# The last quarter of a hand-ordered command list is put in another order

## The chip, the cores and the metric

The kernel runs on one core of a Trainium2 chip. The metric is the device time of one execution in microseconds (us). The engines are TensorE (PE in the rows; its weight loads are PEld), VectorE (DVE), ScalarE (ACT), GpSimd (POOL) and SyncE (SP), which only issues transfers here. Each works through its own queue in the order in which its instructions were written.

## The reference

Sliding-window attention with a few global keys, for 4 batches of 768 positions and 8 heads of 64, and then a two-layer network on all 3072 tokens: 512 to 2048 and back, with h * tanh(softplus(h)) between them.

```python
scores = scale * np.matmul(q, k.transpose(0, 1, 3, 2))
...
scores = np.where(keep, scores + bias, -1e9)     # 8 global keys, or the last 96
a = np.exp(scores - np.max(scores, axis=-1, keepdims=True))
a = a / (np.sum(a, axis=-1, keepdims=True) + 1e-09)
x = np.matmul(a, v)                              # heads side by side: 3072 x 512
...
h = x @ w_in
g = h * np.tanh(softplus(h))
return g @ w_out
```

## The kernel before

The tokens are worked on in 12 chunks of 256 (ci), and the 2048 hidden columns in 8 blocks of 256 (fp). A command of the network has the number m = 8 ci + fp, from 0 to 95; a command of attention has a number t from 0 to 95 (a chunk's eight pairs of heads and blocks of 128 rows). Each number in full precision is split into a high and a low half in fp16, and products are three matmuls. For the later chunks a product of two 2 x 2 block matrices takes seven block products in place of eight, which needs sums of the operands beforehand and a corner afterwards.

The order of everything is written out by hand: a string PROGRAM of 2153 commands, each a letter, a number and sometimes a stroke. A loop at the end of windowed() emits them one after the other under a manual schedule, so that the string gives each engine's queue. Semaphores make an instruction wait for its operands and for a free buffer. A stroke chooses the other of two engines for the command.

The commands that matter here, for one m:

- i (moe_in, L631; for m of 88 and more moe_in_seven, L602): TensorE multiplies weights and tokens. moe_in_seven fills a bank "ph" first and a bank "sc" after it; there are two buffers of each.
- I with 100 + m (corner_h, L612 to L616): a copy (ScalarE; with stroke VectorE) and four sums on VectorE, which end in the bank "sc".
- j, u, n, r (L638, L642, L646, L650): four functions on ScalarE.
- H (times_h, L655), VectorE: multiplies by h, which for m of 88 and more it reads from the bank "sc". With this the bank comes free.
- J (sums_g, L668 to L670): three sums on VectorE; with stroke on GpSimd.
- z (high_g, L154 or L152): the high half of gt on ScalarE; with stroke VectorE. Z (low_g, L158): the low half on GpSimd; with stroke VectorE. A low half reads two tiles in SBUF.
- o (moe_out, L805; for m = 95 L821): TensorE multiplies gt and the second weights.

Operands of later blocks are prepared by P (whole_w, L698: GpSimd, with stroke VectorE), G (sums_w, L705 to L713: VectorE, with stroke GpSimd), e (high halves: ScalarE, with stroke VectorE) and m (low halves, L158: GpSimd, with stroke VectorE). A chunk ends with I (corner, L841 to L847) and Q (evacuate, L870, L878), and Y stores it from SP. In attention s, t, y, g, p are scores, maxima, exponentials and the two halves, X is a DMA transposition (L502) on SP, W the product with v (L525), and R, T, U, V finish the rows.

The command k is checks(i). checks(0) (L911 to L915) and checks(1) (L917 to L919) are five and three small operations of VectorE on statistics; checks(2) is one more; checks(3) sums all of it with a matmul (L924) and five small operations of VectorE; checks(5) follows on the last row.

Of the kernel before, what the change touches and what calls it, by code (L numbers as in the profile page):

```python
# [14 lines left out]
U16 = mybir.dt.uint16  # L15
# [27 lines left out]
def tile_kernel(ctx, tc, qd, kd, qT, kT, v, n, w_in, w_out, out):  # L43
# [27 lines left out]
    with ExitStack() as st:  # L71
        left = windowed(st, tc, locals())
# [35 lines left out]
def windowed(st, tc, loc):  # L108
# [170 lines left out]
    k0 = mt.tile([P, P], F32, name="e", bufs=4)  # L279
# [629 lines left out]
    def checks(i):  # L909
# [75 lines left out]
        t70 p69' q19 J50' g68' X69 z48' I5 t71 Z48 z50 s64 y70 p68 X68 Q5 j52 u52 t64 H51 y64 n52 J51' Z50' g64' o48 z51' c19' r52 i53 j53 o49 H52 p64' u53 x8  # L985
        t65 y65 g70 a19' b19 n53 d19 i54 v9 g65 r53 J52' s66 p70' o50 Z51' X64 H53 z52 t67 j54 p65 J53' u54 t66 o51 n54 y66 s72 i56 Z52 q20 Y5 z53' a20 r54 X65
        Z53 H54 J54 h9 y67 i55 g67' g66 j56 z54 p67' p66' u56 n56 o52 j55 r56 t72 t73 H56 J56 u55 n55 r55 z56 Z54 y71 c20 W64 X70 H55 W65 W68 W69 X67 o53 g71
        i57 i58 o54 R16 p71 Z56' l9 W67 T16' J55 d20' W70 j57 X66 u57 n57 y72 j58 U16 b20 W66 z55' X71 g72 p72 X72 u58 r57 W71 y73 H57 Z55 R17 i59 J57' s74 g73'
        t74 n58 z57 t75 V16 r58 j59 y74 H58 T17' o55 u59 i60 U17 p73 J58 n59 I6 g74 Q6 r59 s76 o56 Z57 q21 y75 j60 u60 t76 H59 n60 J59 y76 V17 r60 p74' o57 z58
        z59 Z58' a21' H60 i62 t77 g76' y77 Y6 p76' j62 s78 i61 t79 X73 u62 c22 g77' y79 n62 b21 X76 r62 p77' t78 g75 d22' j61 X77 u61 J60' Z59' z60' H62 y78 o58  # L990
        W72 o59 X74 n61 r61 g79 Z60' J62' c21' W77 W76 W73 i63 g78 z62 j63 H61 u63 q23 n63 p78 i64 d21' x9 R18 Z62' r63 X78 p75 o60 j64 J61 p79' z61 u64 n64 H63
        s80 t80 a22' J63 Z61 r64 b22 T18 i66 o61 j66 z63 v10 t81 H64 W78 u66 y81 J64' X79 Z63' i65 W79 X75 y80 n66 W74 g80 j65 u65 r66 U18 h10 W75 g81' z64' q22
        p80' o62 p81 n65 H66 Z64 X81 i67 J66' r65 R19 z66 s82 j67 u67 H65 Z66 V18 l10 t82 t83 J65' i68 n67 y82 g82 c24' d24' r67 j68 u68 s84 t85 H67 o63 p82 t84
        I7 i69 y85 Q7 y84 J67' g85 n68 j69 X80 z65 s86 g84 o64 c23 r68 u69 x10 Z65' p85 X85 v11 n69 T19' H68 y83 t86 z67 o65 r69 p84 J68' U19 Z67' H69 z68 i71
        X84 J69 j71 t87 o66 u71 h11 d23 n71 r71 V19 y86 z69' i70 j70 W80 Z68' W85 H71 o67 g86 l11 a24 p86' a23 P8' J71' y87 i72 g83 u70 b24 p83 n70 r70 Z69' z71
        H70 X82 g87' W81 p87 J70' j72 u72 o68 i73 j73 X83 n72 W83 X86 r72 z70 b23 X87 W84 W82 u73 Z71' R20 H72 n73 r73 o69 T20' G8' Z70' i76 j76 J72' W86 u76
        H73 n76 Y7 z72' U20 e8 o70 V20 W87 i74 Z72' R21 s88 J73' r76 z73' Z73 o71 j74 H76 m8' u74 t89 i75 n74 t88 I8' y89 s90 Q8 J76' t91 g89 r74 z76 p89 o72
        t90 Z76 H74 j75 y91 s92 T21' J74 z74' i77 u75 U21 n75 o73 r75 X89 V21 H75 j77 u77 Z74 g91' n77 r77 P9' p91 H77 J75' y88 i78 g88 t93 p88 G9 j78 i79 x11
        t92 o74 y93 z75' u78 y92 X88 n78 g92' Z75' r78 H78 y90 J77' g93' p92 j79 u79 z77 s94 J78' p93' n79 o75 e9 Z77' r79 X92 t94 z78 i80 g90' H79 j80 u80 n80
        m9' r80 Z78' p90 o76 t95 y94 i81 H80 y95 J79 j81 u81 X93 g95 P10 W89 J80 W88 G10 o77 z79 i83 Y8 o78 n81 z80 p95' e10 Z79' m10 r81 o79 H81 j83 u83 Z80'  # L1000
        n83 r83 i82 X95 W92 J81' H83 W93 W95 I9 g94 Q9 z81 J83' p94 X91 j82 i84 u82 P11' n82 X90 r82 R22 Z81' H82 T22 W91 W90 G11' X94 z83 e11 U22 J82' o80 j84
        W94 i85 u84 m11' n84 P12' G12' z82 r84 R23 T23 j85 V22 u85 o81 e12 Z83' U23 H84 i86 Z82' m12' n85 r85 j86 u86 o82 n86 H85 i87 J84' V23 J85' r86 P111'
        z84 z85 G111 e111 Z84' j87 u87 o83 H86 m111' P13' n87 Z85' G13' i89 r87 I189 H87 j89 J86 e13 m13' u89 z86 J87' o84 n89 i88 Z86' I188 r89 o85 H89 z87 i90
        P14 j88 u88 I190' o86 n88 r88 G14' Y9 J89' Z87' H88 i91 o87 e14 j90 u90 n90 r90 m14' I191' z89 Z89' H90 J88' I10' j91 z88 Q10 u91 Z88 J90' i92 Y10 n91
        r91 H91 i93 I192 I193 z90 j92 u92 n92 Z90' r92 H92 o88 F0 P15 j93 G15' u93 e15 J91 k0 o89 i94 J92' z91 o90 m15 n93 z92 I194' r93 j94 Z91' u94 H93 Z92
        J93' n94 r94 i95 I195' o91 H94 o92 j95 u95 z93' n95 J94' r95 k1 Z93' z94' H95 k3 o93 Z94 z95' o94 k2 Z95' o95 I11 Q11 k5 k4
    """
    with tc.manual_schedule(engines={E.DVE, E.Activation, E.Pool, E.PE, E.SP}):
        for c in PROGRAM.split():
# [154 lines left out]
```

## Time and profile before

| | |
|---|---|
| median of 3 runs | 596.11 us (595.25 to 596.85) |
| the profiled execution | 596.82 us, with a span of 595.0 us |
| TensorE busy | 575.7 us, 97% of the span |
| VectorE, ScalarE, GpSimd busy | 526.7, 508.2 and 337.0 us |
| mean granted clock of TensorE | 0.996 |

The span is the time from the first to the last instruction of the trace. "Granted clock" is the share of TensorE's full clock that it had. Matmuls are pipelined and their ends are modelled, so gaps between them are read from the starts and from the waits. A line in brackets behind a row is idle time of the engine before it, and what ended it.

### The profile page before, as it was taken

To read this page: it belongs to the slowest core of one execution; us is meant where nothing else is said; L and a number is where in the kernel's file an instruction comes from. 1 tells how busy PE (TensorE), PEld (TensorE's weight loads), DVE (VectorE), ACT (ScalarE), POOL (GpSimd) and SP (SyncE) were. 2 spreads that over 40 slices of the span, in tenths; PEclk is the share of its full clock that TensorE was granted. 3 is DMA by queue.
4 is the path that set the end of the run, shared out by engine and by line. 5 is a ranking of instruction groups with operands and counts; after the bars stand their busy time and mean duration, and the time that the engine had idled before them with its cause. 6 is when DMAs were issued, how large, how long until landed. Compare 5 with 4: busy or idle time off the path is not lost.

```text
span 595.0 us, 15592 instructions
## 1 busy us (share of the span) xinstructions
PE 575.7 (97%) x5871; PEld 475.5 (80%) x5871; DVE 526.7 (89%) x1300; ACT 508.2 (85%) x1157; POOL 337.0 (57%) x325
## 2 busy tenths in 40 slices
PE   4999999999999999999999999999999999999987
PEld 3887766666767789888889889888889888889975
DVE  5999999989998998986979988798879899999995
ACT  4999999998999999898888878888998689787861
POOL 0125422244757678677574573424847675877972
PEclk9999999999999999999999999999999999999989
DMA  8999886574555355374764672537444133420001
GB/s 248 317 320 228 163 263 193 147 166 112 135 100 114 68 105 126 69 193 99 116 140 104 129 194 55 107 81 188 85 90 106 21 81 75 72 72 3 36 1 40
DMA packets 133263, 73.80 MB, mean 124 GB/s; under 512 B 102176, under 2 KB 123040, under 8 KB 133184
## 3 DMA queue, kind: packets, MB, share of 16 engines
q1 hardware_dynamic: 132752, 72.50, 51.5%
q8 instruction: 47, 0.77, 0.5%
q10 hardware_dynamic: 432, 0.27, 0.2%
q14 instruction: 32, 0.26, 0.1%
HBM read 38.62 MB, written 6.29 MB: 75 GB/s over the span
## 4 chain that ended last, share of the span: by engine, by line
PE 63%; DVE 15%; ACT 14%; issue 3%; POOL 3%; DMA 2%; SPq 0%; DVEq 0%; ACTq 0%; POOLq 0%
PE ph L631 27%; PE pav L805 10%; PE po L805 7%; PE po L821 6%; PE sc L437 5%; ACT A L460 2%; PE sc L525 2%; PE pav L821 2%; ACT e L646 2%; DVE gf L655 2%; DVE gt L158 2%; ACT e L650 1%; ACT e L642 1%; ACT e L638 1%; DVE A L451 1%
## 5 line engine op out<-in xcount | busy, mean ns | idle before, releaser
L631 PE MATMUL ph<-xT,wts 128*128 128x256 f16 x2112 | 243.0, 273 | 1.3 <-DVE gf L655 1.3
L631 PEld LDWEIGHTS <-wts 128*128 128x128 f16 x2112 | 204.0, 98 | 30.5 <-issue 2.4
L805 PEld LDWEIGHTS <-gt 128*128 128x128 f16 x1491 | 143.7, 98 | 20.3 <-issue 2.6
L460 ACT ACTIVATE A<-A,nm 128x232 f32<-128x232 f32 (+1 forms) x192 | 88.2, 461 | 5.7 <-DVE nm L451 5.6
L158 POOL TENSOR_TENSOR gt<-gf,gt 128x896 f16<-128x896 f32 (+1 forms) x40 | 67.8, 1696 | 40.0 <-ACT gt L154 16.6
L158 POOL TENSOR_TENSOR hl<-A,hl 128x512 f16<-128x512 f32 (+1 forms) x41 | 53.0, 1293 | 49.8 <-ACT hl L154 19.0
L638 ACT ACTIVATE e<-ph 128x512 f32<-128x512 f32 x88 | 51.5, 585 | 28.2 <-PE ph L631 28.0
L451 DVE CUSTOM_DVE_ANT_0 A<-sc,mb 128x232 f32<-128x232 f32 (+1 forms) x192 | 63.6, 375 | 11.9 <-PE sc L437 7.5
L655 DVE SCALAR_TENSOR_TENSOR gf<-e,ph 128x512 f32<-128x512 f32 x88 | 60.1, 682 | 13.2 <-ACT e L650 9.4
L158 DVE TENSOR_TENSOR gt<-gf,gt 128x896 f16<-128x896 f32 (+1 forms) x56 | 66.8, 1193 | 5.5 <-ACT gt L154 5.3
L642 ACT ACTIVATE e<-e,ones 128x512 f32<-128x512 f32 x96 | 68.8, 717 | 1.9
L646 ACT ACTIVATE e<-e,part 128x512 f32<-128x512 f32 x96 | 68.6, 714 | 1.5
L805 PE MATMUL pav<-wts,gt 128*128 128x256 f16 x402 | 66.8, 275 | 0.3 <-DVE gt L158 0.3
L154 ACT ACTIVATE gt<-gf 128x896 f16<-128x896 f32 (+1 forms) x65 | 55.8, 861 | 12.1 <-POOL gf L670 9.4
L668 POOL TENSOR_TENSOR gf<-gf 128x128 f32<-128x128 f32 x53 | 36.6, 690 | 45.1 <-DVE gf L655 41.9
L650 ACT ACTIVATE e<-e 128x512 f32<-128x512 f32 x96 | 59.8, 622 | 1.4
L805 PE MATMUL po<-wts,gt 128*128 128x256 f16 x426 | 58.2, 273 | 0.0
L158 POOL TENSOR_TENSOR wts<-ws,wts 128x512 f16<-128x512 f32 x16 | 21.0, 1314 | 64.2 <-DVE wts L152 36.8
L821 PEld LDWEIGHTS <-gt 128*128 128x128 f16 x312 | 29.3, 98 | 31.0 <-issue 0.6
L669 POOL TENSOR_TENSOR gf<-gf 128x256 f32<-128x256 f32 x53 | 45.3, 854 | 4.2
L821 PE MATMUL po<-wts,gt 128*128 128x512 f16 (+1 forms) x204 | 46.2, 376 | 0.0
L670 POOL TENSOR_TENSOR gf<-gf 128x128 f32<-128x128 f32 x53 | 39.8, 751 | 4.2
(221 smaller groups left out, 1088.0 us busy)
## 6 DMA issues: line engine op xcount, KB each, us to landing
qr<-qT SPq DMA_DIRECT2D x24, 256.0 KB, 2.8
wts<-w_in SPq DMA_DIRECT2D x12, 512.0 KB, 7.3
wts<-w_out SPq DMA_DIRECT2D x12, 512.0 KB, 8.2
kr<-kd SPq DMA_DIRECT2D x32, 184.0 KB, 4.2
out<-wr SPq DMA_DIRECT2D x11, 512.0 KB, 3.2
vr<-v SPq DMA_DIRECT2D x10, 512.0 KB, 3.5
vc<-vo SPq DMA_DIRECT2D x15, 192.0 KB, 3.0
wr<-w_in SPq DMA_DIRECT2D x4, 512.0 KB, 5.6
```

What stands on the lines that cost most here:

```text
L154: nc.scalar.activation(out, in_, AF.Copy, scale=scale)
L158: (nc.vector if other else nc.gpsimd).tensor_tensor(out, in_, high, op=ALU.subtract)
L451: nc.vector.tensor_tensor_reduce(out=A[:, j, 0:w], in0=sc[j][:, 0:w], in1=m, scale=-1.0 / (UNIT if ci < CF32 else UNIT * SQ), scalar=3.0e3 ...
L460: nc.scalar.activation(A[:, j], A[:, j], AF.Exp, bias=nm[:, h:h + 1], scale=-1.0, accum_out=rs[:, h:h + 1])
L631: nc.tensor.matmul(ph[:, j, :].rearrange("p (b t) -> p b t", b=2), wv4[:, 2 * fb, x, c * P:(c + 1) * P], xT[:, :, y * NCC + c, :], start=( ...
L638: nc.scalar.activation(mish[m]["e"], mish[m]["h"], AF.Exp, scale=1.0 / (SV * SW), accum_out=esum[:, m:m + 1])
L642: nc.scalar.activation(e, e, AF.Square, bias=ones)
L646: nc.scalar.activation(e, e, AF.Ln, bias=part, scale=SV * SW / SG / 2.0)
L650: nc.scalar.activation(e, e, AF.Exp, scale=-1.0)
L655: nc.vector.scalar_tensor_tensor(gf, mish[m]["e"], SG / (SV * SW), mish[m]["h"], op0=ALU.subtract, op1=ALU.mult, accum_out=gsum[:, m:m + 1])
L805: nc.tensor.matmul(pos[ci][bank][:, side * HN:(side + 1) * HN], gt[:, x, i, :], w[y], start=not begun[ci][bank], stop=n == 2 and ends.get( ...
L821: nc.tensor.matmul(into, gt[:, x, 2 * j + 1 - bank, :], wv4[:, 2 * fb + 1, y, c], start=not begun[ci][bank], stop=last and j == 1 and n == 2)
```

## The change

From the command behind R17 to the end of PROGRAM, 654 commands in 19 lines of the string, the order is another, and so is the engine of 81 commands (their stroke is added or taken away). No command is added or removed, and nothing else in the kernel is touched. checks(0) and checks(1), k0 and k1, stood apart (behind J91 and behind r95); they now stand together behind J94. checks(3) stands ahead of o94 on TensorE, where it stood ahead of o93. The lines that matter (of the 19 on each side):

```diff
--- before
+++ after
@@ -985,25 +985,25 @@ PROGRAM
-    i57 i58 o54 R16 p71 Z56' l9 W67 T16' J55 d20' W70 j57 X66 u57 n57 y72 j58 U16 b20 W66 z55' X71 g72 p72 X72 u58 r57 W71 y73 H57 Z55 R17 i59 J57' s74 g73'
...
-    X84 J69 j71 t87 o66 u71 h11 d23 n71 r71 V19 y86 z69' i70 j70 W80 Z68' W85 H71 o67 g86 l11 a24 p86' a23 P8' J71' y87 i72 g83 u70 b24 p83 n70 r70 Z69' z71
...
-    t92 o74 y93 z75' u78 y92 X88 n78 g92' Z75' r78 H78 y90 J77' g93' p92 j79 u79 z77 s94 J78' p93' n79 o75 e9 Z77' r79 X92 t94 z78 i80 g90' H79 j80 u80 n80
...
-    n83 r83 i82 X95 W92 J81' H83 W93 W95 I9 g94 Q9 z81 J83' p94 X91 j82 i84 u82 P11' n82 X90 r82 R22 Z81' H82 T22 W91 W90 G11' X94 z83 e11 U22 J82' o80 j84
-    W94 i85 u84 m11' n84 P12' G12' z82 r84 R23 T23 j85 V22 u85 o81 e12 Z83' U23 H84 i86 Z82' m12' n85 r85 j86 u86 o82 n86 H85 i87 J84' V23 J85' r86 P111'
-    z84 z85 G111 e111 Z84' j87 u87 o83 H86 m111' P13' n87 Z85' G13' i89 r87 I189 H87 j89 J86 e13 m13' u89 z86 J87' o84 n89 i88 Z86' I188 r89 o85 H89 z87 i90
-    P14 j88 u88 I190' o86 n88 r88 G14' Y9 J89' Z87' H88 i91 o87 e14 j90 u90 n90 r90 m14' I191' z89 Z89' H90 J88' I10' j91 z88 Q10 u91 Z88 J90' i92 Y10 n91
-    r91 H91 i93 I192 I193 z90 j92 u92 n92 Z90' r92 H92 o88 F0 P15 j93 G15' u93 e15 J91 k0 o89 i94 J92' z91 o90 m15 n93 z92 I194' r93 j94 Z91' u94 H93 Z92
-    J93' n94 r94 i95 I195' o91 H94 o92 j95 u95 z93' n95 J94' r95 k1 Z93' z94' H95 k3 o93 Z94 z95' o94 k2 Z95' o95 I11 Q11 k5 k4
+    i57 i58 o54 R16 p71 Z56' l9 W67 T16' J55 d20' W70 j57 X66 u57 n57 y72 j58 U16 b20 W66 z55' X71 g72 p72 X72 u58 r57 W71 y73 H57 Z55 R17 n58 r58 i59 q21
...
+    Z67' o66 c23 H69 x11 i70 J69' u71 g85 n71 z68 P8' p85 Z68' z69 t86 o67 r71 j70 H71 u70 g82' n70 p82' W84 d23' Z69 y87 J71' X85 r70 W80 g87 W81 W85 p87'
...
+    X88 j74 t90 u74 Q8 T21 n74 r74 o72 H74 j75 P9' u75 s92 Z76' n75 J74' r75 y90 t93 z74' y93 y91 U21 H75 g93 i77 o73 p93' i78 j77 u77 n77 J75' Z74' r77 j78
+    t92 H77 o74 X89 i79 u78 z75 V21 n78 r78 g91' y92 g92 G9 Z75' H78 p92' s94 p91 j79 J77' u79 i80 e9 X92 n79 J78' t94 r79 z77' j80 Z77' g90 y94 o75 H79 t95
...
+    Z80 e10 j83 m10' W89 u83 J81' n83 r83 H83 I9 z81 j82 u82 Q9 W93 n82 P11' G11 r82 Z81 X90 H82 W92 W91 J83' z83 X95 i84 i85 W95 J82' e11 R22 X94 j84 T22
+    m11' W90 W94 U22 u84 j85 P12' u85 n84 n85 R23 T23 Z83' o80 G12' U23 r84 z82 H84 J84' o81 Z82' r85 e12 i86 m12' V22 H85 j86 V23 u86 J85' n86 P111' r86
+    z84 o82 G111 Y9 e111 Z84' m111' z85 i87 H86 j87 o83 u87 n87 P13' i89 Z85' I189' r87 G13' e13 H87 J86 J87' m13' z86 j89 o84 u89 n89 Z86 i88 I188' r89
+    P14' j88 z87 G14' H89 o85 u88 n88 i90 I190' o86 Z87' r88 j90 H88 J89' e14 u90 J88 i91 o87 n90 m14' I191' z88 Z88 r90 H90 I10' z89 Q10 j91 i92 u91 n91
+    Z89' J90' r91 I192 H91 j92 o88 F0 u92 z90 P15 n92 Z90 i93 G15 o89 I193' r92 J91' H92 J92' e15 i94 j93 m15' u93 I194 n93 z91 Z91' r93 H93 j94 o90 u94 n94
+    r94 J93' z92 i95 I195' Z92' z93 j95 o91 Z93' u95 Y10 o92 H94 n95 o93 r95 J94 k0 k1 z94 Z94' H95 k2 z95' k3 Z95 o94 o95 I11 Q11 k5 k4
```

## Rows read from the trace of the kernel before

**Rows 1.** The page, busy time and share of the span by engine.
```profile
PE 575.7 (97%) x5871; PEld 475.5 (80%) x5871; DVE 526.7 (89%) x1300; ACT 508.2 (85%) x1157; POOL 337.0 (57%) x325
```
**Rows 2.** Stages: PE, PEld, DVE, ACT, POOL busy; granted clock; DMA.
```profile
540.00:572.70 32.70, 32.09 (x429) 29.93 (x426) 30.89 (x65) 25.94 (x44) 31.18 (x30) 1.00 0.05 18
572.70:575.70 3.00, 0.18 (x5) 0.01 (x1) 2.76 (x7) 1.70 (x4) 1.00 (x1) 1.00 0.00 0
576.30:579.70 3.40, 3.40 (x24) 2.60 (x22) 2.72 (x8) 1.90 (x4) 1.91 (x3) 0.51 0.00 0
```
**Rows 3.** Waits of PEld, 376.9 to 595 us: total, times, longest.
```profile
PEld L602 <- DVE gf L655: 4.1, 4, 3.0
...
PEld L631 <- DVE gf L655: 1.0, 1, 1.0
...
PEld L805 <- DVE gt L158: 0.6, 1, 0.6
PEld L525 <- DMA AT<-hl: 0.6, 1, 0.6
```
**Rows 4.** Timeline, 569 to 576 us: start, duration, engine, line, operation.
```profile
569.24 0.43 DVE L912 TENSOR_SCALAR ind<-osum 128x12 f32<-128x12 f32 x1
...
569.59 0.17 DVE L913 TENSOR_SCALAR ind<-xmax 128x24 f32<-128x24 f32 x1
569.61 2.13 POOL L158 TENSOR_TENSOR vc<-vr,vc 128x1024 f16<-128x1024 f32 x1
...
569.79 2.00 DVE L914 SCALAR_TENSOR_TENSOR ind<-xmax,ind 128x24 f32<-128x24 f32 x1
...
571.78 0.28 DVE L152 TENSOR_SCALAR hl<-ph 128x128 f32<-128x128 f32 x1
...
573.28 0.57 DVE L616 TENSOR_TENSOR sc<-sc,hl 128x384 f32<-128x384 f32 x1
573.75 1.08 DVE L158 TENSOR_TENSOR gt<-gf,gt 128x896 f16<-128x896 f32 x1
...
574.94 0.69 DVE L655 SCALAR_TENSOR_TENSOR gf<-e,sc 128x512 f32<-128x512 f32 x1
...
575.69 0.51 PE L602 MATMUL sc<-xT,wts 128*128 128x128 f16 x6 [2.81 <-DVE gf L655]
```
**Rows 5.** Groups by line and shape, 376.9 to 595 us: busy, mean ns.
```profile
L158 DVE TENSOR_TENSOR gt<-gf,gt 128x896 f16<-128x896 f32 x28 | 36.1, 1289 | 2.8 <-ACT gt L154 2.8
...
L668 DVE TENSOR_TENSOR gf<-gf 128x128 f32<-128x128 f32 x10 | 5.4, 540 | 0.1
...
L669 POOL TENSOR_TENSOR gf<-gf 128x256 f32<-128x256 f32 x28 | 24.3, 868 | 2.2
L158 POOL TENSOR_TENSOR gt<-gf,gt 128x896 f16<-128x896 f32 x11 | 21.7, 1972 | 10.7 <-DVE gt L152 5.6 <-ACT gt L154 5.0
...
L158 POOL TENSOR_TENSOR wc<-vr,wc 128x512 f16<-128x512 f32 x2 | 2.5, 1288 | 4.6 <-ACT wc L154 4.6
```
**Rows 6.** Timeline, single rows from 537 to 589 us.
```profile
537.74 1.23 DVE L698 TENSOR_TENSOR vr<-wts 128x1024 f32<-128x1024 f16 x1
...
544.11 1.21 DVE L158 TENSOR_TENSOR vo<-vr,vo 128x1024 f16<-128x1024 f32 x1
...
547.06 0.50 PE L602 MATMUL ph<-xT,wts 128*128 128x128 f16 x6
...
559.85 1.17 PE L602 MATMUL ph<-AT,vo 128*128 128x128 f16 x18
...
560.04 0.42 DVE L870 SCALAR_TENSOR_TENSOR wr<-po,vr 128x256 f32<-128x256 f32 x1
...
579.85 0.66 DVE L919 TENSOR_SCALAR ind<-gsum 128x95 f32<-128x95 f32 x1
...
585.00 0.69 DVE L158 TENSOR_TENSOR gt<-gf,gt 128x512 f16<-128x512 f32 x1
...
588.02 1.24 PE L821 MATMUL po<-wts,gt 128*128 128x512 f16 x5
```
**Rows 7.** DMA issues: transpositions for attention, count, us to landing.
```profile
AT<-hl SPq DMA_TRANSPOSE x80, 3.1
```

More of the change, by code (lines that the diff above doesn't have):

```diff
@@ L987, in windowed @@
         Z53 H54 J54 h9 y67 i55 g67' g66 j56 z54 p67' p66' u56 n56 o52 j55 r56 t72 t73 H56 J56 u55 n55 r55 z56 Z54 y71 c20 W64 X70 H55 W65 W68 W69 X67 o53 g71
-        i57 i58 o54 R16 p71 Z56' l9 W67 T16' J55 d20' W70 j57 X66 u57 n57 y72 j58 U16 b20 W66 z55' X71 g72 p72 X72 u58 r57 W71 y73 H57 Z55 R17 i59 J57' s74 g73'
-        t74 n58 z57 t75 V16 r58 j59 y74 H58 T17' o55 u59 i60 U17 p73 J58 n59 I6 g74 Q6 r59 s76 o56 Z57 q21 y75 j60 u60 t76 H59 n60 J59 y76 V17 r60 p74' o57 z58
-        z59 Z58' a21' H60 i62 t77 g76' y77 Y6 p76' j62 s78 i61 t79 X73 u62 c22 g77' y79 n62 b21 X76 r62 p77' t78 g75 d22' j61 X77 u61 J60' Z59' z60' H62 y78 o58
@@ L991, in windowed @@
[L991 to L994, printed above, removed]
@@ L995, in windowed @@
-        X84 J69 j71 t87 o66 u71 h11 d23 n71 r71 V19 y86 z69' i70 j70 W80 Z68' W85 H71 o67 g86 l11 a24 p86' a23 P8' J71' y87 i72 g83 u70 b24 p83 n70 r70 Z69' z71
-        H70 X82 g87' W81 p87 J70' j72 u72 o68 i73 j73 X83 n72 W83 X86 r72 z70 b23 X87 W84 W82 u73 Z71' R20 H72 n73 r73 o69 T20' G8' Z70' i76 j76 J72' W86 u76
-        H73 n76 Y7 z72' U20 e8 o70 V20 W87 i74 Z72' R21 s88 J73' r76 z73' Z73 o71 j74 H76 m8' u74 t89 i75 n74 t88 I8' y89 s90 Q8 J76' t91 g89 r74 z76 p89 o72
-        t90 Z76 H74 j75 y91 s92 T21' J74 z74' i77 u75 U21 n75 o73 r75 X89 V21 H75 j77 u77 Z74 g91' n77 r77 P9' p91 H77 J75' y88 i78 g88 t93 p88 G9 j78 i79 x11
@@ L999, in windowed @@
-        t92 o74 y93 z75' u78 y92 X88 n78 g92' Z75' r78 H78 y90 J77' g93' p92 j79 u79 z77 s94 J78' p93' n79 o75 e9 Z77' r79 X92 t94 z78 i80 g90' H79 j80 u80 n80
-        m9' r80 Z78' p90 o76 t95 y94 i81 H80 y95 J79 j81 u81 X93 g95 P10 W89 J80 W88 G10 o77 z79 i83 Y8 o78 n81 z80 p95' e10 Z79' m10 r81 o79 H81 j83 u83 Z80'
-        n83 r83 i82 X95 W92 J81' H83 W93 W95 I9 g94 Q9 z81 J83' p94 X91 j82 i84 u82 P11' n82 X90 r82 R22 Z81' H82 T22 W91 W90 G11' X94 z83 e11 U22 J82' o80 j84
-        W94 i85 u84 m11' n84 P12' G12' z82 r84 R23 T23 j85 V22 u85 o81 e12 Z83' U23 H84 i86 Z82' m12' n85 r85 j86 u86 o82 n86 H85 i87 J84' V23 J85' r86 P111'
@@ new lines, in windowed @@
+        V16 s74 H58 J57 g73 o55 J58' t74 j59 t75 p73 z57' u59 n59 s76 i60 I6' y75 r59 y74 t77 X73 Z57 z58 H59 y77 Q6 j60 g74 a21 v10 o56 T17' p74 J59 t76 U17
+        b21 y76 u60 c21 n60 i61 Z58' r60 V17 g77 j61 s78 a22' o57 z59 p77' g76' Y6 X77 d21 p76 t79 u61 H60 X76 c22 Z59' o58 n61 t78 x9 i62 W76 r61 d22 y78 H61
+        g78 i63 q23 J60 W73 j62 W77 o59 g75 p78 u62 X78 b22 z60' n62 r62 Z60' y79 H62 W72 J61' h10 j63 J62' i64 R18 s80 u63 p75 z62 g79 z61' n63 Z62' q22 p79
+        j64 t80 r63 H63 u64 n64 X74 r64 T18 t81 Z61 y80 H64 o60 i66 J63' l10 X79 j66 W78 U18 X75 W74 u66 z63 i65 g80' n66 p80 o61 Z63 V18 r66 W79 W75 H66 j65
@@ new lines, in windowed @@
+        u65 J64' i67 R19 n65 T19 z64' y81 Z64' g81 s82 t82 p81 o62 j67 x10 U19 u67 o63 r65 X81 H65 J66' t83 s84 I7 y83 n67 g83' a24 z66 J65' V19 i68 z65' Q7 t84
+        Z65' r67 y84 g84' H67 j68 o64 u68 p83 n68 i69 r68 v11 h11 Z66' t85 H68 j69 u69 s86 p84 l11 n69 y85 r69 J67' z67' i71 b24 J68' X84 o65 X80 y82 j71 t87
+        Z67' o66 c23 H69 x11 i70 J69' u71 g85 n71 z68 P8' p85 Z68' z69 t86 o67 r71 j70 H71 u70 g82' n70 p82' W84 d23' Z69 y87 J71' X85 r70 W80 g87 W81 W85 p87'
+        z71 X82 y86 i72 H70 J70 c24 j72 g86 R20 u72 o68 X83 i73 n72 a23 p86' X87 W87 o69 T20 Z71' r72 z70 W83 j73 H72 X86 d24 Y7 u73 U20 b23 n73 W82 W86 Z70'
@@ new lines, in windowed @@
+        G8' i76 e8 R21 j76 V20 s88 r73 u76 J72' z72' H73 t89 m8 n76 r76 t88 y88 y89 g88 Z72' o70 J73' H76 J76' o71 s90 p88' I8 t91 z73 g89 p89 z76 Z73 i74 i75
+        X88 j74 t90 u74 Q8 T21 n74 r74 o72 H74 j75 P9' u75 s92 Z76' n75 J74' r75 y90 t93 z74' y93 y91 U21 H75 g93 i77 o73 p93' i78 j77 u77 n77 J75' Z74' r77 j78
+        t92 H77 o74 X89 i79 u78 z75 V21 n78 r78 g91' y92 g92 G9 Z75' H78 p92' s94 p91 j79 J77' u79 i80 e9 X92 n79 J78' t94 r79 z77' j80 Z77' g90 y94 o75 H79 t95
+        i81 W88 u80 m9 n80 r80 Y8 z78' j81 X93 o76 u81 Z78' o77 X91 P10' H80 p90 g94 i83 p94' y95 J79' z79 n81 o78 g95 r81 G10 J80' p95' Z79' z80 H81 o79 i82
```

## The prediction

> **What bounds the kernel now.** I read the page's busy line first [rows 1]: TensorE (PE) is busy for 575.7 of 595.0 us, VectorE (DVE) for 526.7, so what leaves TensorE's waits as they are can't move the time. The change begins where TensorE starts i59, 376.9 us into the span; of the stages after that, three matter [rows 2]. From 540 to 572.7 us VectorE is busy for 30.89 of 32.70 us and GpSimd (POOL) for 31.18; then TensorE does 0.18 us of work in 3.0 us; then it runs 3.4 us at a granted clock of 0.51, the lower of its two levels (1.2 GHz), after 1.00 in the stages before. Half of those 3.4 us, 1.7, is what the clock costs. The waits come next [rows 3]: the weight loads, which sit ahead of the matmuls, waited for times_h (H, L655) 4.1 us in four places of L602 and 1.0 us in one of L631, 0.6 us for a low half of gt (Z), and 0.6 us for a DMA transposition. That is 6.3 us, with the clock 8.0 us: all that an order can win back here.
>
> The timeline shows where the largest piece, of 3.0 us, comes from [rows 4]. L914, the fourth operation of checks(0), took 2.00 us, its neighbour L913 on the same 24 columns 0.17. It ended at 571.79, GpSimd's subtraction L158 at 569.61 + 2.13 = 571.74. Behind it in VectorE's queue stood I194', Z91' and H93. H93 ran at 574.94, and TensorE's second half of i95, which needs the bank that H93 reads, at 575.69.
>
> **The change, part by part.** The sums are made on the profiled execution: 596.82 us, of which the span is 595.0 and 1.8 lie outside. It is 0.7 us over the median of 596.11; I take the saving off the median.
>
> *The work itself.* The commands are the same, so TensorE's work is too. 81 commands change their engine, about as many one way as the other: Z six to VectorE and seven to GpSimd, z six to VectorE and five to ScalarE, J five to VectorE and eight to GpSimd. With Z at 1.29 us on VectorE and 1.97 on GpSimd [rows 5] and the other kinds so counted, VectorE's total over these 218 us moves by about 1 us. I cost the balance at nothing; what can undo that is the order on VectorE, and that is what I walked.
>
> *checks(0) and checks(1) go behind J94.* In front of I194' 2.7 us are gone: L914 (2.00) and the four beside it (0.7). So H93 comes 2.7 us earlier and the wait of 3.0 us falls to a few tenths. The other waits of rows 3, each of 1.0 us or less, left the clock at 1.00 up to 572.7 [rows 2], so I count the 1.7 us as won too. What is late next is the end: there the eight operations now stand ahead of Z94', H95 and z95', with nothing queued on GpSimd between J93' and Z95. Lower bound eight times L913's 0.17, 1.4 us, less their overlap, 1.2; upper bound 3.8, from L914's 2.00, L919's 0.66, L912's 0.43 [rows 4, 6] and five short ones. I take 1.2: L913 is the row without GpSimd beside it.
>
> The Trainium skill (SBUF — State Buffer, Who interferes with whom) states that a VectorE instruction with two SBUF inputs and a GpSimd one that reads SBUF exclude each other for a whole instruction, and one with a single input is held only in a two-port mode. L914's end just behind L158's agrees. By it the place of the eight is free as long as GpSimd is idle, as in the sum, and dear if it isn't, which is a rival below.
>
> *The end, walked by hand.* From the end of i95 (T) VectorE does the last two sums of I195' (0.9), Z92' and Z93' (1.1 each), H94 with its accumulator (0.8), J94 (three operations, the longest 0.54 [rows 5]: 1.2), the eight (1.2), Z94' (1.1), H95 (0.8), k2 and z95' (0.6): T + 8.8, with handovers 9.0. Z95 goes to GpSimd: 1.29 us on 512 columns, where VectorE took 0.69 [rows 5, 6]. So o95 can start at T + 10.4. TensorE reaches o94 at T + 7.3 (three times 2.3, and the check's matmul), waits for Z94' until T + 7.7, and would reach o95 at T + 10.0. Together 0.8 us; 2.5 at most, with the dearer eight. I take 1.3, as the walk has no contention with J93'. Before, Z95' was done at 585.69 and o95 began at 588.02 [rows 6], so TensorE set this end.
>
> *P14 goes from GpSimd to VectorE, between I188' and H89.* m13' ended at 545.32 [rows 6]. I188' is like I194', 2.1 us from 571.78 to 573.85 [rows 4]; P14' takes 1.23 like P13' [rows 6]; H89 0.7: 549.3. TensorE began i90 at 547.06 and is some 0.5 us earlier now, so it reaches the second half, which needs the bank of Y89, at 547.8. This wait grows from 0.5 to 1.5 us. Bounds 0.5, if VectorE reaches I188' 1 us sooner, and 2.6.
>
> *i93 stands behind o88, and Z89' and I192 ahead of H91.* Q10 ended at 560.46 [rows 6]; Z89' (1.1), I192's four sums (1.7) and H91 (0.7) follow: 564.0. TensorE is through i92 at 559.5 (i93 followed on it at once, its first bank's matmuls at 559.85 [rows 6]), with o88 at 561.8, and at the second half of i93 1.3 us later, 563.2: 0.8 us, 0.3 before. From H91 on VectorE does G15, I193', H92, m15', I194, Z91' and H93: 2.0 + 2.1 + 0.7 + 1.2 + 1.7 + 1.1 + 0.7, to 573.5. TensorE does o89, i94, o90 and half of i95 from 565.1, to 573.4. So i95 waits 0.1 us.
>
> *i85 stands right behind i84 and needs H82*, and on VectorE G11 is now ahead of H82, beside P11' (about 2 us more, an estimate from L698's 1.23 on the larger operand). I take 0.7 us (0 to 1.6), in place of the 1.0 at i86 and the 0.6 for a transposition.
>
> *The rest, i59 to i82.* Before lost 0.6 us, at o75. W85 is now close behind X85, a transposition that lands 3.1 us after its issue [rows 7]: 0 to 0.7 us. Z74' stands right ahead of o74: 0 to 1.0. I take 0.9 for both. Y10 moves back on SP (SyncE), with only the last stores behind it.
>
> *Sum.* Waits after: 0.9 + 0.7 + 1.5 + 0.3 (i92, as before) + 0.8 + 0.1 + 1.3 = 5.6, less 0.4 where an earlier wait lets VectorE catch up: 5.2. 8.0 - 5.2 = 2.8 us less: 596.1 - 2.8 = 593.3 us.
>
> **The rivals.** *Given back.* VectorE is busy for 94% of the stage from 540 us on [rows 2]. If it enters that stage 1.1 us later than I have it (P12' now waits behind G11), the waits at i90 and i93 are 2.6 and 1.3 us, and 1.6 us more is lost: 594.9 us, up to 596.5 with the upper bounds of i85 and o74. For it: GpSimd is as busy, so any of VectorE's sums may be held. Against it: G15 and m15 leave GpSimd.
>
> *The checks on the path: slower.* If GpSimd still works when checks(0) begins, the eight take 3.8 instead of 1.2 us, Z94' and Z95 come 2.6 us later, TensorE idles for some 3 us as at 572.7, and the clock halves as at 576.3 [rows 2], which costs 1.7 us and as much again on the rest of o94 and o95, 1.0: 593.3 + 2.6 + 1.7 + 1.0 = 598.6. It decides from where J93' ends after J94 begins. For it: three J' stand behind Z90 on GpSimd. Against it: H93 lies 6 us of VectorE ahead of checks(0), and J93' takes three operations of at most 0.87 [rows 5].
>
> *Less contention: better.* With P14, G15, m15 and Z92 off GpSimd, it holds fewer of VectorE's operations. The 28 Z' took 1.29 us on average [rows 5], the one at 573.75 took 1.08 [rows 4]; seven Z', and the J and P as well, would give VectorE 2 us in the last stage, and the waits at i90 and i93 go, 2.2 us: 591.1. The Trainium skill's page has it that whichever starts first holds the ports; by that rule this comes about if GpSimd's queue empties.
>
> **How the numbers follow.** Forecast 0.45 (592.0 to 594.9), given back 0.27, less contention 0.15, the checks on the path 0.13. The predicted time is 593.3. The range 590.3 to 597.7 leaves out the slower case and the far end of the better one, under 2 in 10. A measurement of this kernel can tell 0.3%, 1.8 us. Below 594.3 lie most of the forecast (0.38), less contention (0.15) and a little of the second case (0.04): faster 0.57. Same is the rest of these, 0.30; slower 0.13.
>
> **What would show it.** The 3.0 us wait of i95 and the stage at 0.51 should be absent; L914 should last under 0.3 us; TensorE should wait for H89, for H91 and, at the end, for Z94' or Z95, each under 1.6 us. The prediction is wrong if a gap of TensorE passes 2.5 us, if L914 is long in its new place, or if new waits before 512 us exceed 2 us.

## The result and the profile after

| | before | after |
|---|---|---|
| median | 596.11 us | 591.05 us (590.39 to 591.81) |
| ratio, 95% interval | 1 | 0.992 (0.990 to 0.994) |
| the profiled execution, span | 596.82, 595.0 us | 591.81, 590.0 us |
| mean granted clock | 0.996 | 1.000 |

The change makes the kernel 5.1 us faster, where 2.8 us were forecast. The time lies inside the range, but outside the 592.0 to 594.9 us of the forecast case, and nearest to the rival of less contention. The page's busy line of after answers to [rows 1]:

```profile
PE 573.9 (97%) x5866; PEld 475.2 (81%) x5871; DVE 519.4 (88%) x1290; ACT 510.7 (87%) x1163; POOL 339.4 (58%) x329
```

TensorE is busy for 1.8 us less with the same commands, close to the 1.7 us put down to the stage at half clock. VectorE is busy for 7.3 us less, which was not forecast. The stages of after answer to [rows 2] (start and end; busy time of PE, PEld, DVE, ACT, POOL; granted clock; DMA):

```profile
540.00:570.00 30.00, 29.23 (x390) 27.39 (x389) 27.93 (x64) 24.06 (x41) 23.60 (x25) 1.00 0.05 19
570.00:573.50 3.50, 3.41 (x53) 3.15 (x51) 3.19 (x7) 3.40 (x8) 2.78 (x4) 1.00 0.00 0
573.50:586.00 12.50, 12.50 (x113) 9.94 (x110) 11.74 (x34) 5.85 (x9) 1.75 (x3) 1.00 0.00 1
```

The stage of 3 us with an idle TensorE is gone, and so is the one at 0.51. From 540 us on GpSimd is busy for 79% of the stage, where it was 95% before. In the 12.5 us from 573.5 on, in which the eight checks now run, GpSimd does 1.75 us of work and TensorE never stops.

The weight loads' waits from 376 to 590 us (total, times, longest), which answer to [rows 3]:

```profile
PEld L525 <- DMA AT<-hl: 1.1, 3, 0.5
...
PEld L602 <- DVE gf L655: 0.7, 2, 0.4
PEld L602 <- issue: 0.6, 1, 0.6
```

The 4.1 us for times_h in L602 are down to 0.7, the 1.0 in L631 and the 0.6 for a low half are gone, and the transpositions cost 0.5 us more. The 0.6 us under "issue" are the wait at i93, which ends when H91 does. Read from one matmul to the next, TensorE now has five gaps over 0.2 us: 0.39 and 0.41 at W76 and W94, 0.42 at i90, 0.68 at i93 and 0.25 at i95, in sum 2.15 us. Read in the same way, before has 6.0.

The two places that [rows 4] showed are here in the timeline of after (start, duration, engine, line, operation; in brackets idle time before it):

```profile
571.59 0.69 DVE L655 SCALAR_TENSOR_TENSOR gf<-e,sc 128x512 f32<-128x512 f32 x1
...
572.35 0.51 PE L602 MATMUL sc<-xT,wts 128*128 128x128 f16 x6
...
578.17 0.17 DVE L912 TENSOR_SCALAR ind<-osum 128x12 f32<-128x12 f32 x1
578.24 0.17 DVE L913 TENSOR_SCALAR ind<-xmax 128x24 f32<-128x24 f32 x1
...
578.45 0.18 DVE L914 SCALAR_TENSOR_TENSOR ind<-xmax,ind 128x24 f32<-128x24 f32 x1
...
578.99 0.20 DVE L919 TENSOR_SCALAR ind<-gsum 128x95 f32<-128x95 f32 x1
579.25 1.09 DVE L158 TENSOR_TENSOR gt<-gf,gt 128x896 f16<-128x896 f32 x1
...
580.33 0.45 PE L924 MATMUL sc<-ind,ones 128*1 128x171 f32 x2
...
580.72 0.50 PE L805 MATMUL pav<-wts,gt 128*128 128x256 f16 x3
...
581.62 1.16 POOL L158 TENSOR_TENSOR gt<-gf,gt 128x512 f16<-128x512 f32 x1 [7.45 <-DVE gt L152]
...
583.02 1.46 PE L821 MATMUL po<-wts,gt 128*128 128x512 f16 x6
```

H93 ends at 572.28 and the second half of i95 starts at 572.35. L914 takes 0.18 us, where it took 2.00, and L912 0.17, where it took 0.43; no operation of GpSimd stands beside them. Z94' ends at 580.34, o94 follows the check's matmul at 580.72, Z95 ends at 582.78 and o95 starts at 583.02, when TensorE gets to it.

### The profile page after: what moved, and what is told of

It is laid out like the page before. It is cut to its first block, busy times and chain, and to the rows that moved or that the text cites. A ratio compares the mean times of both kernels' runs of the same rounds, so it can differ in the third digit from the quotient of the medians.

```text
span 590.0 us, 15598 instructions
## 1 busy us (share of the span) xinstructions
PE 573.9 (97%) x5866; PEld 475.2 (81%) x5871; DVE 519.4 (88%) x1290; ACT 510.7 (87%) x1163; POOL 339.4 (58%) x329
## 4 chain that ended last, share of the span: by engine, by line
PE 76%; DVE 10%; ACT 5%; DMA 5%; issue 2%; POOL 1%; SPq 1%; DVEq 0%; ACTq 0%; POOLq 0%
PE ph L631 34%; PE pav L805 12%; PE po L805 9%; PE po L821 7%; PE sc L437 5%; PE pav L821 4%; PE sc L525 3%; DMA AT<-hl 2%; ACT A L460 1%; DVE gf L655 1%; DVE gt L158 1%; DMA qr<-qT 1%; DMA kr<-kd 1%; DVE A L451 1%; PE pav L525 1%
## 5 line engine op out<-in xcount | busy, mean ns | idle before, releaser
L631 PE MATMUL ph<-xT,wts 128*128 128x256 f16 x2112 | 243.1, 273 | 0.1
L631 PEld LDWEIGHTS <-wts 128*128 128x128 f16 x2112 | 203.9, 98 | 29.2 <-issue 1.9
L158 POOL TENSOR_TENSOR gt<-gf,gt 128x896 f16<-128x896 f32 (+1 forms) x41 | 68.4, 1668 | 43.5 <-ACT gt L154 14.5
L158 POOL TENSOR_TENSOR hl<-A,hl 128x512 f16<-128x512 f32 (+1 forms) x40 | 51.2, 1280 | 56.5 <-ACT hl L154 23.0
L158 DVE TENSOR_TENSOR gt<-gf,gt 128x896 f16<-128x896 f32 (+1 forms) x55 | 65.0, 1183 | 4.4 <-ACT gt L154 4.0
L668 POOL TENSOR_TENSOR gf<-gf 128x128 f32<-128x128 f32 x56 | 41.5, 741 | 29.6 <-DVE gf L655 25.2
L158 POOL TENSOR_TENSOR wts<-ws,wts 128x512 f16<-128x512 f32 x16 | 20.6, 1289 | 64.1 <-ACT wts L154 25.6
L669 POOL TENSOR_TENSOR gf<-gf 128x256 f32<-128x256 f32 x56 | 49.9, 891 | 4.4
L670 POOL TENSOR_TENSOR gf<-gf 128x128 f32<-128x128 f32 x56 | 42.2, 753 | 4.4
```

What stands on the lines that cost most here:

```text
L158: (nc.vector if other else nc.gpsimd).tensor_tensor(out, in_, high, op=ALU.subtract)
L631: nc.tensor.matmul(ph[:, j, :].rearrange("p (b t) -> p b t", b=2), wv4[:, 2 * fb, x, c * P:(c + 1) * P], xT[:, :, y * NCC + c, :], start=( ...
```

## The experiments

Ratios are to the kernel before, run on the same chip, with the 95% interval.

### The checks alone: checks(0) moved in before, and moved back in after

```diff
-    ... u93 e15 J91 k0 o89 i94 J92' ...
+    ... u93 e15 J91 o89 i94 J92' ...
-    ... n95 J94' r95 k1 Z93' ...
+    ... n95 J94' r95 k0 k1 Z93' ...
```

> The kernel before with one edit: checks(0) stands right ahead of checks(1), behind r95, and no longer behind J91. Theory A (the 3.0 us wait of i95 came from checks(0) being held up beside GpSimd, and the half clock came from that wait): the wait of i95 falls under 0.5 us, no stage at 0.51, and 2.7 + 1.7 = 4.4 us go, less up to 0.7 us in the new place, where J94' runs on GpSimd: 591.7 to 592.5 us. Rival B (the order of the whole last quarter is what counts; VectorE is 94% busy there and the wait turns up again at H93, o93 or o94): 594 us or more.

Measured: 592.80 us against 596.02, 0.994 (0.9925 to 0.9956). The granted clock of the profiled execution is 1.00, TensorE waits 0.79 us at i95, 1.4 us at i86, and L914 takes 0.62 in its new place, beside a sum on GpSimd. The time is 0.3 us above the range expected, and the wait at i95 above its 0.5. So this one move brings 3.2 us (2.6 to 4.5 by the interval) of the 5.1. The other way round, after with k0 put back to where before has it, between m15' and I194:

```diff
-    ... i94 j93 m15' u93 I194 ...
+    ... i94 j93 m15' k0 u93 I194 ...
-    ... r95 J94 k0 k1 z94 ...
+    ... r95 J94 k1 z94 ...
```

> The changed kernel with one edit: checks(0) stands behind m15' and ahead of I194, where GpSimd still has J91' and J92' to do; checks(1) stays. Theory A: L914 takes 1 us or more, H93 comes 1.5 to 2.5 us later, TensorE waits 1.5 to 2.7 us in i95; 592.6 us if the clock holds, 594.5 us if it halves again. Rival B: the order around it has the room, at most 591.6 us.

Measured: 592.74 us against 596.02, 0.9939 (0.9923 to 0.9955). The second half of i95 waits again, 1.85 us from one matmul to the next, and the clock stays at 1.00. But in the timeline of this kernel it isn't L914 that is long:

```profile
568.83 0.42 DVE L911 TENSOR_SCALAR ind<-osum 128x22 f32<-128x22 f32 x1
...
569.24 0.44 DVE L913 TENSOR_SCALAR ind<-xmax 128x24 f32<-128x24 f32 x1
...
569.82 0.70 DVE L915 TENSOR_SCALAR ind<-wmax 128x2 f32<-128x2 f32 x1
...
574.02 0.51 PE L602 MATMUL sc<-xT,wts 128*128 128x128 f16 x6 [1.68 <-DVE gf L655]
```

L915 handles two columns with a single input and took 0.70 us, where it takes 0.16 behind J94. The time came out as expected, its place did not: which of the five is long depends on where GpSimd is, not on the operation.

### Is L914 the culprit? It alone left out

This kernel leaves out the upper bound on xmax, the only one of the five with two inputs.

```diff
-            nc.vector.scalar_tensor_tensor(ind[:, 3 * NC - 2:NA - 1], xmax, XMOST, ...)
```

> The kernel before without L914, the one operation that took 2.00 us (the upper bound on xmax is left out; the rest of checks(0) stays where it is). Theory A: H93 comes 1.8 to 2.0 us earlier, i95 waits about 1.1 us, and the clock stays at 1.00: 596.1 - 1.9 - 1.7 = 592.5 us. Rival B: another operation of VectorE is held up in its place, since GpSimd is busy throughout: 595 us or more.

Measured: 595.94 us against 596.02, 0.9993 (0.9981 to 1.0005): no change, and the theory with which I came, that two-input operations are what is held, falls; the rival that the expectation named holds. The next one, on wmax (L914 is its line in this kernel), took its place:

```profile
570.44 2.14 POOL L158 TENSOR_TENSOR vc<-vr,vc 128x1024 f16<-128x1024 f32 x1
570.51 2.10 DVE L914 TENSOR_SCALAR ind<-wmax 128x2 f32<-128x2 f32 x1
```

It began 0.07 us behind GpSimd's subtraction and ended 0.03 us behind it. So I took that one out of the way as well: as above, and the operation on wmax moved to the front of checks(1).

```diff
         if i == 0:
...
-            nc.vector.scalar_tensor_tensor(ind[:, 3 * NC - 2:NA - 1], xmax, XMOST, ...)
-            nc.vector.tensor_scalar(ind[:, NA + NG:NA + NG + 2 * NFP:NFP], wmax, 1.0, ...)
         elif i == 1:
+            nc.vector.tensor_scalar(ind[:, NA + NG:NA + NG + 2 * NFP:NFP], wmax, 1.0, ...)
```

> As the earlier kernel without L914 (the upper bound on xmax is left out), where the next operation, on wmax, took the 2.1 us in its place; here that one goes to checks(1) as well, so that the copy of I194' from PSUM is what follows L913 on VectorE. Theory A, sharpened (any of VectorE's operations that stays within SBUF is held while GpSimd subtracts, one that reads PSUM is not): I194' starts at once, i95 waits 1.0 us, the clock stays at 1.00, 592.6 us. Rival: I194' is held as well, 595.9 us.

Measured: 592.57 us against 595.43, 0.9952 (0.9937 to 0.9968). What VectorE starts behind GpSimd's subtraction is now the copy from "ph" (I194'), which reads PSUM:

```profile
569.45 2.14 POOL L158 TENSOR_TENSOR vc<-vr,vc 128x1024 f16<-128x1024 f32 x1
569.51 0.28 DVE L152 TENSOR_SCALAR hl<-ph 128x128 f32<-128x128 f32 x1
...
573.42 0.51 PE L602 MATMUL sc<-xT,wts 128*128 128x128 f16 x6 [0.69 <-DVE gf L655]
```

It has GpSimd beside it for its whole length and takes 0.28 us. In [rows 4] it took as much, but there L158 began 0.03 us behind it; the same copy with GpSimd idle, in after at 564.21, took 0.28 as well. With the two runs together: a small operation of VectorE that begins behind GpSimd's subtraction and whose operands all lie in SBUF was held until that ended, with two inputs (L914) or one (wmax); the one that reads PSUM was not. That is no rule for every operation within SBUF. L918, on a single column, went through beside a sum on GpSimd in the kernel before:

```profile
579.70 0.74 POOL L669 TENSOR_TENSOR gf<-gf 128x256 f32<-128x256 f32 x1
...
579.78 0.15 DVE L918 TENSOR_SCALAR ind<-worst 128x1 f32<-128x1 f32 x1
```

The Trainium skill bears this out: SBUF — State Buffer, Who interferes with whom, counts tensor_scalar among the operations that can take the shared ports, and VectorE: DVE Perf Modes, Mode 2×_2P — use both read ports for one tensor, asks for operands in SBUF for it. The traces agree, with 2.10 us for two columns within SBUF and 0.28 us for 128 from PSUM.

### The clock: the gap of before filled with work

The first products of i95 ("ph") are made three times over, each writing over the last, so that TensorE has work while it waits for H93.

```diff
-            for q, (kx, kw) in enumerate(products):
+            for q, (kx, kw) in list(enumerate(products)) * (3 if m == NC * NFP - 1 and name == "ph" else 1):
```

> The kernel before, with the products of i95 that go to the bank ph made three times over (the later ones overwrite the same values), so that TensorE works through 2.6 of the 3.0 us in which it waited for H93. H93 itself is where it was. If the half clock came from the idle TensorE, it stays at 1.00 and 1.7 us go: 594.4 us. If the clock falls for another reason: 596.1 us and a stage at 0.51.

Measured: 594.87 us against 596.02, 0.998 (0.9969 to 0.9992). The stages of the gap and behind it:

```profile
572.00:576.20 4.20, 4.19 (x74) 4.01 (x72) 3.89 (x10) 2.46 (x6) 2.27 (x2) 1.00 0.00 0
576.20:580.00 3.80, 3.67 (x43) 3.40 (x44) 3.46 (x12) 2.61 (x5) 2.44 (x5) 1.00 0.02 4
```

H93 comes no sooner, and yet 1.15 us are won: the stage at 0.51 is gone when TensorE does not stand idle in front of it. One profile shows one execution; over all of them the mean granted clock was 0.998 or more in 12 of 12 here, and 0.997 or less in 16 of 23 of before. The interval reaches from 0.5 to 1.8 us, so the 1.7 us read from the profile is not refuted.

### The halves of the change

Before up to i89 and the order and engines of after from there:

```diff
 (up to i89 as before)
-    ... i89 r87 I189 H87 j89 J86 e13 m13' ...
+    ... i89 I189' r87 e13 H87 J86 J87' m13' ...
 (to the end as after)
```

> The kernel before up to i89 (537.8 us), and from there the remaining commands in the changed kernel's order and with its engines. Theory A (of the 5 us, 3.2 are checks(0), as its move alone showed, and most of the rest lies ahead of i89, where the waits of i86, W94 and o75 went): these three waits stay, 591.05 + 1.1 = 592.1 us. Rival B (the rest lies in the last 50 us): 591.1 us.

Measured: 592.70 us against 595.43, 0.9954 (0.994 to 0.9968). The gaps at o75, W94, i86, i90, i93 and i95 are 0.50, 0.77, 0.63, 0.83, 0.68 and 0.24 us, 3.65 in all against 2.15 of after. The time is 0.6 us above the one expected. Such sums are those of one execution: the gap at i86 alone lies between 0.59 and 1.42 us in the six profiles with this order ahead of it. The reverse, after up to P13' and the rest as before:

```diff
 (up to P13' as after)
-    ... i89 Z85' I189' r87 G13' e13 H87 J86 J87' m13' ...
+    ... Z85' G13' i89 r87 I189 H87 j89 J86 e13 m13' ...
 (to the end as before)
```

> The changed kernel up to i89, and from there the remaining commands in the order and with the engines of the kernel before, checks(0) at its old place. Theory A: the waits of i86, W94 and o75 shrink by 1.1 us, the 3.0 us wait of i95 and the half clock stay: 594.9 us. Rival B: 596.0 us, or more.

Measured: 595.32 us against 595.43, 0.9982 (0.9968 to 0.9996). The gaps before 540 us shrink to 0.36, but i92 waits 1.05 and i95 2.59 us, and then the clock falls:

```profile
572.40:574.60 2.20, 0.11 (x2) 0.00 (x0) 2.06 (x4) 1.38 (x3) 0.55 (x1) 1.00 0.00 0
574.70:578.00 3.30, 3.06 (x24) 2.75 (x25) 1.99 (x8) 1.32 (x2) 1.64 (x3) 0.50 0.00 0
```

The gaps come to 4.6 us in all, 1.4 less than before's, and the ratio's interval reaches from 0.2 to 1.9 us. The median of 0.1 us alone would say less than that, as the half clock (a mean of 0.997 or less) was in 6 of the 12 executions here and in 10 of before's 23; those with it take 595.58 us for before's 596.52, those without 593.53 for 595.08. So this half is worth some 0.9 to 1.6 us, which agrees with its gaps and with the 1.5 us by which the gaps of the other half alone exceed those of after.

### The order at i93

Could the wait at i93 be saved by i93 going back ahead of o88?

```diff
-    ... I192 H91 j92 o88 F0 u92 z90 P15 n92 Z90 i93 G15 ...
+    ... I192 H91 i93 j92 o88 F0 u92 z90 P15 n92 Z90 G15 ...
```

> The changed kernel with i93 ahead of o88, as it stood before the change, nothing else moved. TensorE reaches the second half of i93 2.3 us sooner and H91, at 562.1, stays where it is: a wait of some 3 us in place of 0.7 there, and at the end 2.3 us more if nothing catches up, 593.3 us; with a half clock behind a gap of that length 595 us. Rival: the 2.3 us are won back behind it, since o88 then covers the next wait: at most 591.6 us.

Measured: 594.73 us against 595.43, 0.9983 (0.9971 to 0.9994). The wait grows to 2.98 us, and the stage behind it is at half clock:

```profile
562.54 0.68 DVE L655 SCALAR_TENSOR_TENSOR gf<-e,sc 128x512 f32<-128x512 f32 x1
...
563.28 0.51 PE L602 MATMUL sc<-xT,wts 128*128 128x128 f16 x6 [2.82 <-DVE gf L655]
...
563.80:567.30 3.50, 3.50 (x25) 2.75 (x23) 2.95 (x9) 3.47 (x6) 2.21 (x2) 0.51 0.00 0
```

H91 begins at 562.54 here and at 562.09 in after; the order of TensorE hardly moves it. o88 in front of i93 is 2.3 us of work in the place of a wait.

### The waits that are left: P14 back on GpSimd, and two H sooner

Both were run beside another run of after.

> The changed kernel as it is, once more, so that the two edits of it are compared on one chip: 590.4 to 591.1 us, with a granted clock of 1.00 throughout.

Measured: 590.85 us against 596.45, 0.9923 (0.9902 to 0.9945).

```diff
-    P14' j88 z87 G14' H89 ...
+    P14 j88 z87 G14' H89 ...
```

> The changed kernel with P14 back on GpSimd (the stroke taken away). The prediction's step (P14' ahead of H89 on VectorE lengthens the wait of i90): H89 comes 1.3 us sooner, the wait of 0.4 us there goes, 0.4 us less than the changed kernel. Rival: P14 takes 2.1 to 2.9 us on GpSimd, G14' and J89' come 1 to 1.5 us later and hold VectorE's J88 and m14' up; H90 comes later and i92 waits 0.5 to 1 us: 0.3 to 0.8 us more than the changed kernel.

Measured: 592.00 us, 0.9935 (0.9917 to 0.9954), 1.15 us slower than after. The gap at i90 falls from 0.66 (this second run of after) to 0.27, as wanted; but now i92 waits:

```profile
551.75 1.06 ACT L154 ACTIVATE vc<-vr 128x1024 f16<-128x1024 f32 x1 [1.37 <-POOL vr L713]
...
555.10 1.89 POOL L158 TENSOR_TENSOR gt<-gf,gt 128x896 f16<-128x896 f32 x1 [0.44 <-ACT gt L154]
...
557.02 0.69 DVE L655 SCALAR_TENSOR_TENSOR gf<-e,sc 128x512 f32<-128x512 f32 x1 [0.69 <-POOL gt L158]
...
557.77 0.51 PE L602 MATMUL sc<-xT,wts 128*128 128x128 f16 x6 [1.10 <-DVE gf L655]
```

H writes a tile "gf", of which there are two buffers. H90 can't start until Z88 has read the one it gets, and Z88 on GpSimd ends at 556.99. Z88 did not stand in GpSimd's queue: it waited 0.44 us for its high half z88 on ScalarE. That stands behind e14, the first row, which waited 1.37 us for the last sum of G14' on GpSimd; behind P14 this sum ended at 551.72, in the second run of after at 549.19. So Z88 comes later, and H90, the bank and i92 come later with it. Now the two H that TensorE waits for are put ahead of the work that stands in front of them:

```diff
-    P14' j88 z87 G14' H89 o85 ...
-    Z89' J90' r91 I192 H91 j92 ...
+    H89 P14' j88 z87 G14' o85 ...
+    Z89' J90' r91 H91 I192 j92 ...
```

> The changed kernel with H89 ahead of P14' and H91 ahead of I192 on VectorE, which are the two largest waits of TensorE that are left in the last 50 us (0.4 us at i90, 0.7 at i93). If these waits are on the path: 0.6 to 1.0 us less than the changed kernel. Rival: I192, G14' and what hangs on them come 0.7 us later, the waits turn up again at i94 or i95, and nothing is won.

Measured: 592.90 us, 0.9949 (0.9932 to 0.9967), 2.05 us slower than after. The gaps at i90 and i93 shrink to 0.27 and 0, and larger ones open at i92 (1.14) and i94 (1.37), with smaller ones at i91 (0.40) and i95 (0.38). The one at i94 hangs on a buffer again:

```profile
565.65 1.89 POOL L158 TENSOR_TENSOR gt<-gf,gt 128x896 f16<-128x896 f32 x1 [2.94 <-ACT gt L154]
...
567.58 0.69 DVE L655 SCALAR_TENSOR_TENSOR gf<-e,sc 128x512 f32<-128x512 f32 x1 [0.88 <-POOL gt L158]
...
568.33 0.51 PE L602 MATMUL sc<-xT,wts 128*128 128x128 f16 x6 [1.21 <-DVE gf L655]
```

Z90 ends at 567.54 and H92 starts at 567.58. GpSimd had been idle for 2.94 us before Z90: its high half z90 stands on ScalarE behind j92, and j92 waited 3.52 us (2.37 in the second run of after) for the sums of I192, which now come behind H91. None of the kernels tried is faster than after.

## Why the prediction was right, and where its sum was off

*The main piece held.* That L914 stood behind GpSimd's subtraction, that the 3.0 us at i95 and the half clock hang on it, and that both go when the checks move behind J94, is shown by the run that moves checks(0) alone (3.2 us), and by the run that fills the gap. The eight took 1.1 us in their new place, 578.09 to 579.19, for 1.2 in the sum; the wait at i95 is 0.25 for 0.1. But the two inputs of L914 were half of the explanation: without L914, wmax's single-input operation was held for 2.10 us. Nor was L913 a row without GpSimd beside it, as the sum had it: L158 ran from 569.61 on, 0.02 us behind L913's start. The price was right for the kernel as it stood; for leaving L914 out it was wrong by 3.4 us, in the expectation above.

*The end: 0 for 1.3 us.* From the end of i95, at 573.53, I had Z95 ready at T + 10.4 and o94 late by 0.4. Measured: H94 ends at T + 3.5, J94 at T + 4.6, Z94' at T + 6.8, z95' at T + 7.9 and Z95 at T + 9.2; TensorE comes to o95 at T + 9.5. The step that failed is the walk's addition: T + 9.0 for z95' adds up whole durations with handovers on top, and in the trace an operation starts before the recorded end of the one ahead of it (578.17, 578.24, 578.45 for operations of 0.17). H's accumulator starts within H as well (576.98; H94 ends at 577.05). That made 1.1 us in 20 operations, more than the 0.8 of the walk, and the 0.5 that I had put on top for contention with J93' was not needed either: GpSimd did nothing from 574.17 to 581.62.

*i90: 0.42 for 1.5 us.* (The "bank of Y89" in the prediction is the one that H89 reads.) The step that failed is "m13' ended at 545.32", taken from before. In after VectorE is 1.03 us ahead, and the timeline has:

```profile
543.08 1.21 DVE L158 TENSOR_TENSOR vo<-vr,vo 128x1024 f16<-128x1024 f32 x1
...
546.19 1.34 DVE L698 TENSOR_TENSOR vr<-wts 128x1024 f32<-128x1024 f16 x1
...
547.46 0.67 DVE L655 SCALAR_TENSOR_TENSOR gf<-e,sc 128x512 f32<-128x512 f32 x1
...
548.20 0.51 PE L602 MATMUL sc<-xT,wts 128*128 128x128 f16 x6 [0.26 <-DVE gf L655]
```

This is the lower bound that I had named, VectorE 1 us sooner, and I did not take it because I let TensorE profit from the earlier stages (0.5 us) and VectorE not. Of the 1.03 us 0.70 are there when H87 begins (540.83 for 541.53): m111' (1.22 us on VectorE) now stands ahead of H86 and not behind it. The other 0.3 is J86, whose first sum took 0.39 us for 0.71. No run changes either alone. P14' itself costs 1.34 for the 1.23 in the sum. And I had it as a cost only: back on GpSimd the time is 1.15 us longer, since G14', e14, z88 and so Z88 come later there.

*i93: 0.68 for 0.8 us.* H91 ends at 562.77, 1.2 us sooner than forecast, and TensorE is about as much sooner. With i93 in its old place the wait is 2.98 us, so the move is needed with this order of VectorE.

*i85, i92 and the early part: 0.80 for 1.9 us.* i85 waited for nothing, as H82 was ready (517.63 to 518.32; i85 began at 518.53); what is left there of the 0.7 is 0.41 for the transposition ahead of W94. i92 waited 0 for 0.3. The 0.9 for W85 and o74 became 0.39 at W76: a transposition, but another one.

*The balance of the engines.* I costed it at nothing, since the counts shift by about 1 us. From 376 to 590 us, before and then after:

```profile
376.00:590.00 214.00, 209.12 (x2318) 184.12 (x2315) 190.16 (x423) 170.75 (x354) 141.68 (x137) 0.99 0.32 70
376.00:590.00 214.00, 208.70 (x2342) 184.37 (x2338) 185.49 (x417) 173.91 (x361) 144.38 (x141) 1.00 0.32 72
```

VectorE has 4.7 us less in a stretch in which after does its work to the end. Added up operation by operation, from the start of i59 to the end of each kernel, it is 6.8 us: 424 operations and 212.5 us before, 414 and 205.7 after. Half of that, 3.4 us, is the count alone, at the mean durations of before, where I had about 1 us: work left VectorE. The first sum of J, for one, ran there ten times before [rows 5] and seven times after. 1.8 us are L914, and 1.7 are other operations that took less; 1.0 of these are the Z' on VectorE, 28 as before, at 1.25 us each for 1.29 [rows 5]:

```profile
L158 DVE TENSOR_TENSOR gt<-gf,gt 128x896 f16<-128x896 f32 x28 | 35.0, 1253 | 1.8 <-ACT gt L154 1.5
...
L668 DVE TENSOR_TENSOR gf<-gf 128x128 f32<-128x128 f32 x7 | 2.3, 326 | 0.1
```

So the rival of less contention came true in small part. Of the two waits that it named, i93 kept its own, and i90's shrank with VectorE's lead, of which 0.3 us is a sum that took less.

*The sum.* I had 8.0 us to win from the weight loads' waits (6.3) and the clock (1.7), and 5.2 us lost again in after. Read by the gaps on both sides, before loses 6.0 and after 2.15. The forecast had 3.05 us too much in after: 1.3 at the end, 1.1 at i90, 1.1 at i85, i92 and the early part and 0.1 at i93, less 0.15 at i95 and the 0.4 that I had taken off for catching up. Gaps and clock then make 5.6 us; from the start of i59 to the last matmul the profiled executions differ by 5.3 (214.2 and 208.8 us) and the medians by 5.1. The missing 0.3 to 0.5 us may be the clock: I counted its 1.7 as lost in every execution of before, and 34 of 58 had it. That is not settled.

That the time came out within 0.1 us of the rival's 591.1 is luck: its 2.2 us were to come from i90 and i93, and those two brought 1.2. Of the 5.1, the move of checks(0) has 3.2 by the run on it alone and the part up to i89 some 0.9 to 1.6; the rest is within what these runs can tell. Putting k0 back costs only 1.7 to 1.9, where the stop it makes is 1.85 us instead of 2.98 and the clock stays at 1.00.

## What to carry to other kernels

When one engine's short operation is long in the trace, look at what the neighbour on its ports does at that moment and move the operation to where the neighbour is idle; taking out the one that happened to be caught only hands the wait to the next. A wait that TensorE has for an operation of VectorE is a wait on a loop of buffers: before moving that operation forward, follow what frees the buffer it writes, and what the reader of that buffer waits for in its turn (here a low half on GpSimd, which waited for its high half on ScalarE). In a walk by hand, carry an engine's lead into the next stage for all engines or for none.

## What the runs showed of the hardware that was not expected

- A VectorE operation on 128x2 with one input took 2.10 us beside a GpSimd subtraction, and 0.16 without; one on 128x128 from PSUM took 0.28 in both cases. One on a single column within SBUF took 0.15 with GpSimd beside it and without.
- The clock did not follow the length of a gap alone. After TensorE had done next to nothing for 2.98 us (before, and with i93 ahead of o88) and for 2.59 us (the head alone) the next stage was at 0.50 to 0.51; after 2.87 us, in the profiled execution without L914, it stayed at 1.00, though 7 of that kernel's 12 executions had a mean of 0.997 or less:

```profile
573.40:576.40 3.00, 0.34 (x6) 0.16 (x3) 2.76 (x7) 1.65 (x4) 1.14 (x1) 1.00 0.00 0
576.40:580.00 3.60, 3.56 (x42) 3.31 (x43) 3.21 (x9) 2.43 (x5) 2.41 (x4) 1.00 0.00 0
```

- Nor did it come in every execution of one kernel: of 58 of before, 34 had a mean granted clock of 0.997 or less, and the other 24 were 0.9 to 2.2 us shorter (medians, in three series of runs). A mean of 0.998 is no sign of it: the profiled execution without L914 has that from the time behind 592.14 us alone, when TensorE is done. One profile is not enough to price it.
